# Up weights of two units loaded together by rows, and up products of the last 128 tokens over 512 columns at a time

## The chip, the cores and the metric

The kernel runs on one core of one Trainium2 chip. The metric is device time in microseconds (us), the median of repeated runs. Before the change it is 1033.2 us (three runs, 1032.21 to 1035.63). A profiled execution is a run of its own, with its own time.

## The reference

Attention with a linear memory, then a softplus feed-forward layer, then a mixture of eight experts whose gates are balanced by Sinkhorn rounds. All of it is in fp32.

```python
x = attention(q, k, v, M_prev, z_prev, beta)      # 1152 tokens x 512
g = softplus(x @ w_in)                            # w_in 512 x 2048
x = g @ w_out                                     # 1152 x 512
P = sinkhorn(x @ w_gate)                          # 1152 x 8, eight rounds
for e in range(8):
    h = np.maximum(x @ w1[e], 0.0)                # w1[e] 512 x 1024
    out += P[:, e:e + 1] * (h @ w2[e])            # w2[e] 1024 x 512
```

## The kernel before, in words

Each fp32 operand is split in two fp32r parts: a high part (`...h`, copied and rounded by ACT) and a low part (`...l`, the rest, subtracted by DVE). A product takes three matmuls: high by high, high by low, low by high.

The 1152 tokens are three chunks, 512, 512 and 128. The two chunks of 512 go together through a Strassen form of seven block products (`product`, L1264: 42 matmuls of 512 columns in a unit); their weights are the four blocks a11, a21, a12, a22 of a unit and four sums s1 to s4 of these. The last chunk, 128 tokens, is done plainly (`plain`, L1285): its tokens are the stationary side, and the weights are the moving side.

The experts' work is a list of units. An expert has two halves `s`; a half has two up units (`what` = 2s and 2s+1, each for 256 hidden columns) and one down unit that uses the hidden values of both. `up2` does an up unit: products of A, C and B in turn, and between them ACT's copies of A (`keep`, L1327) and DVE's additions of C to them (L1331). `plain` stands between the third product and the fourth and fifth, and writes its unit's 256 columns of the PSUM bank `po`; after the second unit of a half `hidden` (L1309) copies the bank, transposes it and splits it.

Weights come in by `load_pair` (L1147): one DMA of 512 KB into one of two `raw` buffers, then four jobs: split of row 0 (a11, a21), sums s1 and s2 (POOL) and their split, split of row 1 (a12, a22), sums s3 and s4 and their split. A unit's load stands LOOK = 3 units ahead in a list of jobs (`pump_q`), from which `pump()` takes one between products. A split part lies in a `slot` of 128x512, out of a ring of W0 + W1 = 27 (the first 16 in use from the start, 11 more after the attention), taken in order and free when the last matmul has read it.

Nothing of this order is fixed by hand: `Plan` lists every instruction with what it reads and writes, and a list scheduler places them, engine by engine, with the planner's own cost for each. The engines then run their queues in that order and wait on semaphores.

Of the kernel before, what the change touches and what calls it, by code (L numbers as in the profile page):

```python
# [19 lines left out]
P = 128  # L20
# [6 lines left out]
E = 8  # L27
# [10 lines left out]
GROUPS = [list(range(n, n + 4)) for n in range(0, 16, 4)]  # L38
AT = (14, 16, 18, 20)
AO = (34, 36, 38, 39)  # L40
W0, W1 = 16, 11
HT, HG, HH, HU, HS = 4, 8, 12, 8, 2
LOOK = 3
YIELD = 80
# [46 lines left out]
        self.ap = pool.tile(self.shape, self.dtype, name=self.name, **kw)  # L91


class Op:
    __slots__ = ("eng", "ns", "fn", "rank", "wait", "outs", "ready", "allocs", "touch", "start", "lat", "end", "port", "kind")


class Plan:
# [17 lines left out]
    def add(self, eng, ns, fn, r=(), w=(), lat=0, rank=None, after=(), port=False, kind=None):  # L116
        o = Op()
        o.eng, o.ns, o.fn, o.lat, o.port, o.kind = eng, ns, fn, lat, port, kind
        self.rank += 1
        o.rank = self.rank + self.shift if rank is None else rank  # L120
        o.outs, o.ready, o.allocs, o.touch, deps = [], 0, [], {}, set(after)
        for bufs, write in ((r, False), (w, True)):
            for b in bufs:
                b, sub = b if isinstance(b, tuple) else (b, None)
                for s, p, pw in b.log:
                    if p is not o and (write or pw) and (
                            s is None or sub is None or s == sub or s[0] != sub[0]):
                        deps.add(p)
                b.log.append((sub, o, write))
                if write and b not in o.allocs:  # L130
                    o.allocs.append(b)
                    if b.pool in self.gates:
                        deps.add(self.gates[b.pool])
                o.touch[b] = True
        o.wait = len(deps)
        for p in deps:
            p.outs.append(o)
        self.ops.append(o)
        return o
# [111 lines left out]
def fused_kernel(ctx, tc, kq, vq, gm, w_in, w_out, wg, w1, w2, out1, out2):  # L251
# [22 lines left out]
    def pe(ns, fn, r, w, **kw):  # L274
        return pl.add("PE", ns, fn, r, w, kind=kw.pop("kind", "all"), **kw)
# [11 lines left out]
    def dma(kb, fn, w, r=(), late=0, **kw):  # L287
        return pl.add("SP", max(460, kb * 2.8), fn, r, w, lat=2000 + late + kb * 2.8, **kw)
# [27 lines left out]
    pl.banks["slot"] = [(None, ("w", f"w{n}")) for n in range(W0)]  # L316

    def slot(name):
        return pl.any_buf("slot", [P, 512], F32R, name)

    def load_split64(src, name, after=(), psum=False, keep=False):
        raw = pl.buf("d", [P, 512, 2], U32, "raw64", "raw")
        a = pl.buf("psb", [P, 512], F32, "cv", "b5") if psum else pl.buf("d", [P, 512], F32, "wa", "wa")
        hi, lo = slot(name + "h"), slot(name + "l")
# [32 lines left out]
    def sum_moe1(g, k):  # L359
# [12 lines left out]
        op(s12, R, s12, L, one, L, ALU.subtract)  # L372
        op(s34, R, two, L, s12, R, ALU.subtract)
        for n, t in enumerate((s12, s34)):
            hi, lo = slot(f"s{g}{k}{n}h"), slot(f"s{g}{k}{n}l")
# [769 lines left out]
    wa_, wb_, wd_ = {}, {}, {}  # L1145

    def load_pair(src, e, i, order, rows, table):  # L1147

        box = []
        at = {name: slice(n * 256, (n + 1) * 256) for n, name in enumerate(order)}  # L1150

        def two(ap, read, name, lo_eng):
            hi, lo = slot(name + "h"), slot(name + "l")
            copy(512, lambda: hi.ap, ap, read, [hi])
            pair(512, lambda: lo.ap, ap, lambda: hi.ap.bitcast(F32), ALU.subtract, [*read, hi], [lo], eng=lo_eng)
            return hi, lo

        def load():
            raw = pl.buf("d", [P, 1024], F32, "raw", "raw")
            box.append(raw)  # L1160
            dma(512, lambda: nc.sync.dma_start(raw.ap, src[e, i]), [raw])

        def row(r):
            raw = box[0]
            hi, lo = two(lambda: raw[:, r * 512:(r + 1) * 512], [raw], f"a{e}{i}{r}", "DVE")
            if rows is not None:
                rows[e, i + 4 * r] = hi, lo
            for m in range(2):
                table[e, i, order[2 * r + m]] = hi, lo, m

        def sums(r):
            raw = box[0]
            t = pl.buf("d", [P, 512], F32, "ws", "wa")

            def op(m, x, y, o, rd):
                pair(256, lambda: t[:, m * 256:(m + 1) * 256], x, y, o, rd, [t])

            def a(name):
                return lambda: raw[:, at[name]]

            if r == 0:
                op(0, a("a21"), a("a22"), ALU.add, [raw])
                op(1, lambda: t[:, 0:256], a("a11"), ALU.subtract, [raw])
                box.append(t)
            else:
                q = box[1]
                op(0, a("a11"), a("a21"), ALU.subtract, [raw])
                op(1, a("a12"), lambda: q[:, 256:512], ALU.subtract, [raw, q])
            hi, lo = two(lambda: t.ap, [t], f"s{e}{i}{r}", "DVE")
            for m in range(2):  # L1190
                table[e, i, f"s{2 * r + m + 1}"] = hi, lo, m

        return [load, lambda: row(0), lambda: sums(0), lambda: row(1), lambda: sums(1)]

    def load_unit(n):
        e, s, what = units[n]
        if what != "down":
            return load_pair(w1, e, what, ("a11", "a21", "a12", "a22"), None, wa_)
        two = [load_pair(w2, e, i, ("a11", "a21", "a12", "a22"), wb_, wd_) for i in (2 * s, 2 * s + 1)]
        return [f for fs in two for f in fs]  # L1200

    pr = pl.buf("cst", [P, NTT, E], F32, "pr")

# [80 lines left out]

    def plain(o, e, i):  # L1285


        n = i % 2
        out = slice(n * 256, (n + 1) * 256)

        def step(k):
            wh, wl, _ = wa_[e, i, "a1%d" % (k // 2 + 1)]
            h, l = xh[2], xl[2]

            def cols(w):
                return w.ap.rearrange("p (r k f) -> p k r f", r=2, k=2)[:, k % 2]

            def mm():
                kw = {"skip_group_check": True} if n else {}
                nc.tensor.matmul(o[:, out], h[:, k, :], cols(wh), start=(n + k == 0), stop=False, **kw)  # L1300
                nc.tensor.matmul(o[:, out], h[:, k, :], cols(wl), start=False, stop=False, **kw)
                nc.tensor.matmul(o[:, out], l[:, k, :], cols(wh), start=False, stop=(k == KD - 1), **kw)

            pe(3 * mms(256), mm, [wh, wl, h, l], [o])

        for k in range(KD):
            step(k)

    def hidden(o):  # L1309
# [226 lines left out]
def _layout(q, k, v, M_prev, z_prev, beta, moe_w_in, moe_w_out, moe2_w_gate, moe2_w1, moe2_w2):  # L1536
# [16 lines left out]
    for j in range(2):  # L1553
# [12 lines left out]
        "wg": c(moe2_w_gate.reshape(KD, P, E).transpose(1, 0, 2)),  # L1566


        "w1": c(moe2_w1.reshape(E, 2, 2, P, 2, NF2 // 2, P).transpose(0, 5, 3, 1, 4, 2, 6)).reshape(E, NF2 // 2, P, 1024),
# [21 lines left out]
```

## Time and profile before

| | |
|---|---|
| median of the runs | 1033.2 us |
| the profiled execution, its own time | 1032.61 us |
| its span, first to last instruction | 1030.8 us |
| PE / DVE / ACT / POOL busy | 1017.0 / 916.8 / 593.6 / 342.7 us |
| attention and start of the first layer | 0 to about 125 us |
| feed-forward layer | about 125 to 310 us |
| experts | about 310 us to the end |

The busy time of PE (matmuls) is drawn from modelled ends: a 512-column matmul is shown as 0.39 us long while the next one starts 0.227 us later. What a matmul takes of PE is therefore read from the starts of successive matmuls. The clock column PEclk gives the granted share of TensorE's full clock; 1.00 is 2.4 GHz.

### The profile page before, as it was taken

To read this page: it belongs to the slowest core of one execution; us is meant where nothing else is said; L and a number is where in the kernel's file an instruction comes from. 1 tells how busy PE (TensorE), PEld (TensorE's weight loads), DVE (VectorE), ACT (ScalarE), POOL (GpSimd) and SP (SyncE) were. 2 spreads that over 40 slices of the span, in tenths; PEclk is the share of its full clock that TensorE was granted. 3 is DMA by queue.
4 is the path that set the end of the run, shared out by engine and by line. 5 is a ranking of instruction groups with operands and counts; after the bars stand their busy time and mean duration, and the time that the engine had idled before them with its cause. 6 is when DMAs were issued, how large, how long until landed. Compare 5 with 4: busy or idle time off the path is not lost.

```text
span 1030.8 us, 14822 instructions
## 1 busy us (share of the span) xinstructions
PE 1017.0 (99%) x5270; PEld 836.0 (81%) x5270; DVE 916.8 (89%) x1722; ACT 593.6 (58%) x1200; POOL 342.7 (33%) x360
## 2 busy tenths in 40 slices
PE   7999999999999999999999999999999999999998
PEld 5777787888877888888888888888888888888886
DVE  7998877767668999999999999999999999999987
ACT  6888877766756764546454553545545344553542
POOL 3424351313343233433323333242432323343220
PEclk9999999999999999999999999999999999999999
DMA  4340222332201112211111211211211121111102
GB/s 167 126 152 26 87 82 82 103 102 102 103 21 41 42 56 59 62 62 61 62 41 53 71 42 62 62 41 42 73 50 41 62 62 62 40 54 62 41 2 92
DMA packets 27021, 68.38 MB, mean 66 GB/s; under 512 B 2556, under 2 KB 11332, under 8 KB 26948
## 3 DMA queue, kind: packets, MB, share of 16 engines
q1 hardware_dynamic: 26948, 67.45, 20.0%
q8 instruction: 41, 0.67, 0.3%
q14 instruction: 32, 0.26, 0.1%
HBM read 65.04 MB, written 2.40 MB: 65 GB/s over the span
## 4 chain that ended last, share of the span: by engine, by line
PE 93%; DVE 3%; ACT 3%; issue 1%; DMA 0%; ACTq 0%; DVEq 0%
PE pa L1276 6%; PE pa L1277 6%; PE pa L1278 6%; PE dA L1451 6%; PE dA L1450 6%; PE dA L1452 6%; PE pc L1278 3%; PE pc L1276 3%; PE pc L1277 3%; PE dn L919 3%; PE dn L918 3%; PE dn L917 3%; PE dC L1451 3%; PE dC L1450 3%; PE dC L1452 3%; PE xp L683 2%
## 5 line engine op out<-in xcount | busy, mean ns | idle before, releaser
L284 POOL TENSOR_TENSOR ws<-raw 128x256 f32<-128x256 f32 x128 | 122.8, 959 | 450.0 <-issue 104.5
L279 ACT ACTIVATE fh<-u 128x512 fp32r<-128x512 f32 x160 | 99.3, 628 | 121.7 <-DVE u L1376 65.5
L285 DVE TENSOR_TENSOR fl<-u,fh 128x512 fp32r<-128x512 f32 x160 | 110.9, 694 | 1.9 <-ACT fh L279 1.8
L1327 ACT ACTIVATE u<-pa 128x512 f32<-128x512 f32 x64 | 38.0, 593 | 66.4 <-PE pa L1278 65.9
L1467 DVE TENSOR_TENSOR acc<-dA,acc 128x512 f32<-128x512 f32 x92 | 62.3, 681 | 4.9 <-PE dA L1452 4.8
L1347 ACT ACTIVATE pb<-pa 128x512 f32<-128x512 f32 x32 | 18.6, 582 | 78.8 <-PE pa L1278 53.1
L284 POOL TENSOR_TENSOR ws<-raw,ws 128x256 f32<-128x256 f32 x64 | 61.8, 966 | 0.0
L279 ACT ACTIVATE fh<-t 128x512 fp32r<-128x512 f32 x64 | 38.6, 624 | 37.3 <-DVE t L1376 37.3
L284 POOL TENSOR_TENSOR ws<-ws,raw 128x256 f32<-128x256 f32 x64 | 57.3, 896 | 4.9
L1331 DVE TENSOR_TENSOR u<-pc,u 128x512 f32<-128x512 f32 x64 | 43.9, 686 | 7.6 <-ACT u L1327 5.5
L285 DVE TENSOR_TENSOR fl<-t,fh 128x512 fp32r<-128x512 f32 x64 | 47.3, 740 | 0.0
L1340 DVE SCALAR_TENSOR_TENSOR u<-u,pb 128x512 f32<-128x512 f32 x56 | 42.5, 759 | 0.6
L1467 DVE TENSOR_TENSOR acc<-dC,acc 128x512 f32<-128x512 f32 x62 | 40.1, 679 | 0.3
L593 ACT ACTIVATE pr<-pr,mn 128x128 f32<-128x128 f32 (+3 forms) x64 | 35.6, 560 | 7.5 <-DVE mn L578 7.3
L279 ACT ACTIVATE pt<-tp 128x512 f32<-128x512 f32 (+3 forms) x72 | 31.2, 451 | 6.6 <-PE tp L607 6.2
L570 PE MATMUL sp<-st 64*128 64x256 f32 (+2 forms) x192 | 26.7, 383 | 6.6 <-ACT st L279 5.1
L683 PE MATMUL xp<-pt,vt 128*64 128x128 f32 (+2 forms) x480 | 32.1, 265 | 0.0
L284 POOL TENSOR_TENSOR gl<-u,gh 128x512 fp32r<-128x512 f32 x12 | 15.5, 1295 | 49.1 <-ACT u L844 49.1
L578 DVE CUSTOM_DVE_ANT_0 pr<-sp,mask 128x128 f32<-128x128 f32 (+3 forms) x64 | 29.6, 483 | 2.3 <-PE sp L570 2.0
L607 PE MATMUL tp<-ident,pr 128*128 128x128 f32 x160 | 28.9, 290 | 1.8 <-DVE pr L624 0.8
L333 DVE SCALAR_TENSOR_TENSOR cv<-cv,raw 128x512 uint32<-128x512 uint32 x24 | 16.7, 696 | 15.7 <-ACT raw L331 15.7
L284 POOL TENSOR_TENSOR st<-kqd,st 128x640 fp32r<-128x640 f32 (+1 forms) x14 | 21.2, 1529 | 23.6 <-ACT st L279 23.6
(5131 smaller groups left out, 3600.7 us busy)
## 6 DMA issues: line engine op xcount, KB each, us to landing
raw<-w SPq DMA_DIRECT2D x64, 512.0 KB, 3.4
raw<-w_in SPq DMA_DIRECT2D x16, 512.0 KB, 3.5
raw<-w_out SPq DMA_DIRECT2D x16, 512.0 KB, 3.5
vt<-vq SPq DMA_DIRECT2D x8, 608.0 KB, 4.0
kqd<-kq SPq DMA_DIRECT2D x7, 608.0 KB, 4.1
pb<-gates SPq DMA_DIRECT2D x16, 256.0 KB, 5.1
out<-acc SPq DMA_DIRECT2D x9, 256.0 KB, 2.0
gms<-gm SPq DMA_DIRECT2D x2, 260.0 KB, 6.1
```

The lines of the kernel that those rows point to most:

```text
L279: return act(n, lambda: nc.scalar.activation(out(), src(), AF.Copy), r, w, x=-42 if psum else 0, **kw)
L284: return gps(n, lambda: nc.gpsimd.tensor_tensor(out=out(), in0=a(), in1=b(), op=op), r, w, **kw)
L285: return dve(n, lambda: nc.vector.tensor_tensor(out=out(), in0=a(), in1=b(), op=op), r, w, port=True, **kw)
L683: nc.tensor.matmul(xp[j * D:(j + 1) * D, P - R:P], vt[:kk, t * P + j * D:t * P + (j + 1) * D], src, start=False, stop=(t == nb - 1), skip_ ...
L1276: nc.tensor.matmul(o[:, :CH], wh[:, at], h(), start=start and k == 0, stop=False, **kw)
L1277: nc.tensor.matmul(o[:, :CH], wh[:, at], l(), start=False, stop=False, **kw)
L1278: nc.tensor.matmul(o[:, :CH], wl[:, at], h(), start=False, stop=(k == 1), **kw)
L1331: dve(CH, lambda: nc.vector.tensor_tensor(out=t.ap, in0=o[:, :CH], in1=t.ap, op=ALU.add), [o], [t], rank=pl.rank - FORE)
L1450: nc.tensor.matmul(o[:, :CH], wh[:, at], h.ap, start=start and n == 0, stop=False, **kw)
L1451: nc.tensor.matmul(o[:, :CH], wh[:, at], l.ap, start=False, stop=False, **kw)
L1452: nc.tensor.matmul(o[:, :CH], wl[:, at], h.ap, start=False, stop=(n == 1), **kw)
L1467: dve(CH, lambda: nc.vector.tensor_tensor(out=acc[c][:, cs_], in0=o[:, :CH], in1=acc[c][:, cs_], op=ALU.add), [o], [a_])
```

## The change

The up weights of a half (two units) are laid out by rows: one 512 KB DMA brings a row block (a11, a21 or a12, a22) of both units. `load_up` issues the two DMAs at the first unit; each unit then has its own four jobs, so both `raw` buffers stay in use until the second unit's last job. The down weights are loaded as before, by `load_down`.

The ring has tiles of 128x1024: W0 = 8 and W1 = 5, 13 doubles in place of 27 singles. For up rows a double holds the high (or the low) part of one row for both units, and becomes free only when both units are done with it; for sums, down rows and the first layer's weights it holds high and low part of one row. `Half` lets the planner treat the two halves apart when it looks for dependencies.

`plain` runs over 512 columns, those of both units: two of the four k steps in the first unit and two in the second (for the first half of the first expert all four in the second unit). A half's 24 matmuls of 256 columns become 12 of 512, with a moving operand of four pieces of 128 columns, where there were two.

```diff
-W0, W1 = 16, 11
+W0, W1 = 8, 5
...
     def slot(name):
-        return pl.any_buf("slot", [P, 512], F32R, name)
+        return pl.any_buf("slot", [P, 1024], F32R, name)
+
+    def two_parts(name):
+        s = slot(name)
+        return Half(s, 0), Half(s, 1)
...
+    def load_up(e, s):
+        raws = []
 
         def load():
-            raw = pl.buf("d", [P, 1024], F32, "raw", "raw")
-            box.append(raw)
-            dma(512, lambda: nc.sync.dma_start(raw.ap, src[e, i]), [raw])
+            for r in range(2):
+                load_raw(raws, w1[e, s, r])
+                wp_[e, s, r] = slot(f"a{e}{s}{r}h"), slot(f"a{e}{s}{r}l")
+
+        def row(n, r):
+            i = 2 * s + n
+            hi, lo = [Half(w, n) for w in wp_[e, s, r]]
+            parts_of(lambda: raws[r][:, n * 512:(n + 1) * 512], [raws[r]], hi, lo)
+            for m in range(2):
+                wa_[e, i, BLOCKS[2 * r + m]] = hi, lo, m
...
+            return [lambda: row(n, 0), lambda: sums_of(e, 2 * s + n, 0, raws, blk, kept, wa_),
+                    lambda: row(n, 1), lambda: sums_of(e, 2 * s + n, 1, raws, blk, kept, wa_)]
+
+        return [[load, *unit(0)], unit(1)]
...
     def plain(o, e, i):
...
-            wh, wl, _ = wa_[e, i, "a1%d" % (k // 2 + 1)]
+            wh, wl = wp_[e, i // 2, k // 2]
             h, l = xh[2], xl[2]
 
             def cols(w):
-                return w.ap.rearrange("p (r k f) -> p k r f", r=2, k=2)[:, k % 2]
+                return w.ap.rearrange("p (q k f) -> p k q f", q=4, k=2)[:, k % 2]
 
             def mm():
-                kw = {"skip_group_check": True} if n else {}
-                nc.tensor.matmul(o[:, out], h[:, k, :], cols(wh), start=(n + k == 0), stop=False, **kw)
...
+                nc.tensor.matmul(o.ap, h[:, k, :], cols(wh), start=(k == 0), stop=False)
...
-        for k in range(KD):
+        for k in (() if i == 0 else range(KD)) if e == 0 and i < 2 else range(i % 2 * 2, i % 2 * 2 + 2):
             step(k)
```

The planner then places everything anew. Up to the feed-forward layer's last group the order on PE is as it was. Two places of the experts follow, both in the first half of expert 3 (numbers behind names are buffer numbers).

PE in the first unit, before: the last three rows of `plain` (`po`), what follows them, and the first rows of the a22 product (`pa` written from a301).

```order
L1300 MATMUL po_6727<-a301h_6443,xh2_1445 128x256
L1301 MATMUL po_6727<-a301l_6468,xh2_1445 128x256
L1302 MATMUL po_6727<-a301h_6443,xl2_1459 128x256
L1276 MATMUL pa_6750<-xh0_287,a310h_6487 128x512
L1277 MATMUL pa_6750<-xl0_300,a310h_6487 128x512
L1278 MATMUL pa_6750<-xh0_287,a310l_6524 128x512
L1276 MATMUL pa_6518<-xs20h_2421,a301h_6443 128x512
L1277 MATMUL pa_6518<-xs20l_2473,a301h_6443 128x512
L1278 MATMUL pa_6518<-xs20h_2421,a301l_6468 128x512
```

The same place now: the last three rows of `plain` in this unit (of six), and what follows.

```order
L1346 MATMUL po_6504<-a300h_6150,xh2_1441 128x512
L1347 MATMUL po_6504<-a300l_6169,xh2_1441 128x512
L1348 MATMUL po_6504<-a300h_6150,xl2_1455 128x512
L1327 MATMUL pa_6325<-xs20h_2412,a301h_6231 128x512
L1328 MATMUL pa_6325<-xs20l_2463,a301h_6231 128x512
L1329 MATMUL pa_6325<-xs20h_2412,a301l_6265 128x512
L1327 MATMUL pc_6426<-xh1_497,s301_6274 128x512
L1328 MATMUL pc_6426<-xl1_505,s301_6274 128x512
L1329 MATMUL pc_6426<-xh1_497,s301_6274 128x512
```

The three matmuls of the next unit (a310) that stood between `plain` and the a22 product have moved away, and twelve short `plain` rows are now six long ones.

DVE where the same unit's `pc` is added to the copy `u3` (L1331 before), before: what stands in front of the addition, and behind.

```order
L285 TENSOR_TENSOR a310l_6716<-raw_6586,a310h_6711 128x512
L1340 SCALAR_TENSOR_TENSOR u1_6725<-pb_6599,pb_5606 128x512
L285 TENSOR_TENSOR s310l_6731<-ws_6693,s310h_6718 128x512
L1331 TENSOR_TENSOR u3_6738<-pc_6571,u3_6738 128x512
L1340 SCALAR_TENSOR_TENSOR u3_6738<-u3_6738,pb_6445 128x512
L285 TENSOR_TENSOR a311l_6767<-raw_6586,a311h_6733 128x512
```

The same place now (L1377 is the addition).

```order
L1513 TENSOR_TENSOR acc0_2365<-dA_6240,acc0_2365 128x512
L299 TENSOR_TENSOR a310_6489<-raw_6381,a310_6489 128x512
L1377 TENSOR_TENSOR u3_6508<-pc_6426,u3_6508 128x512
L299 TENSOR_TENSOR s310_6495<-ws_6469,s310_6495 128x512
L1386 SCALAR_TENSOR_TENSOR u3_6508<-u3_6508,pb_6245 128x512
L299 TENSOR_TENSOR fl_6523<-u1_6471,fh_6477 128x512
```

A split of down weights (a310) stands directly in front of the addition now, and the split of s310 behind it, where both stood in front of it.

## Rows read from the trace of the kernel before

**Rows 1.** Page, part 1: busy us, share of the span, instructions of each engine.

```profile
span 1030.8 us, 14822 instructions
PE 1017.0 (99%) x5270; PEld 836.0 (81%) x5270; DVE 916.8 (89%) x1722; ACT 593.6 (58%) x1200; POOL 342.7 (33%) x360
```

**Rows 2.** Page, part 4: the chain that ended last, by engine.

```profile
PE 93%; DVE 3%; ACT 3%; issue 1%; DMA 0%; ACTq 0%; DVEq 0%
```

**Rows 3.** Stretches (us), busy us and instructions by engine, PEclk, DMA share, GB/s.

```profile
0.00:125.00 125.00, 115.41 (x1039) 86.56 (x1040) 110.72 (x436) 102.08 (x307) 45.53 (x56) 1.00 0.34 115
125.00:290.00 165.00, 164.49 (x762) 135.38 (x760) 119.60 (x188) 117.01 (x214) 55.30 (x51) 1.00 0.27 91
290.00:420.00 130.00, 129.83 (x620) 105.56 (x619) 114.91 (x223) 76.86 (x138) 44.63 (x45) 1.00 0.17 49
420.00:1000.00 580.00, 580.00 (x2729) 486.03 (x2729) 548.08 (x842) 287.23 (x524) 197.20 (x209) 1.00 0.16 52
```

**Rows 4.** Waits of PE, 125 to 1031 us: us in total, times, longest.

```profile
PE pa L821 <- ACT pb L853: 0.5, 1, 0.5
PE dA L1451 <- DVE fl L285: 0.2, 1, 0.2
```

**Rows 5.** The stretch 290 to 1031 us, line L1300 alone: PE and weight loads.

```profile
290.00:1031.00 741.00, 36.40 (x128) 24.40 (x128) 1.00 0.16 53
```

**Rows 6.** PE in order of time, around one plain block: start, length, line.

```profile
468.80 0.39 PE L1276 MATMUL pa<-xh,s131h 128*128 128x512 f32 x1
...
470.16 0.28 PE L1300 MATMUL po<-a130h,xh 128*128 128x256 f32 x1
...
471.60 0.40 PE L1276 MATMUL pa<-xs20h,a131h 128*128 128x512 f32 x1
```

**Rows 7.** Page, part 6: weight loads, count, KB, us to landing.

```profile
raw<-w SPq DMA_DIRECT2D x64, 512.0 KB, 3.4
```

**Rows 8.** Waits of the DMA queue, 420 to 1000 us.

```profile
SPq L1161 <- DVE a421l L285: 23.0, 2, 11.9
```

**Rows 9.** Tile a420l: who writes and reads it, first and last start.

```profile
L285 DVE TENSOR_TENSOR a420l<-raw,a420h x2: 674/679/684, 691.2 to 719.2; 128x512 fp32r<-128x512 f32 x2
...
L1278 PE MATMUL pa<-xh,a420l x2: 389/389/389, 703.1 to 703.8; 128*128 128x512 f32 x2
```

**Rows 10.** PE in order of time, another plain block.

```profile
558.35 0.39 PE L1278 MATMUL pa<-xh,s231l 128*128 128x512 f32 x1
558.58 0.28 PE L1300 MATMUL po<-a230h,xh 128*128 128x256 f32 x1
...
560.01 0.40 PE L1276 MATMUL pa<-xs20h,a231h 128*128 128x512 f32 x1
```

**Rows 11.** ACT at the same place.

```profile
558.84 0.60 ACT L1327 ACTIVATE u<-pa 128x512 f32<-128x512 f32 x1
```

**Rows 12.** DVE at the same place.

```profile
559.23 0.69 DVE L285 TENSOR_TENSOR fl<-u,fh 128x512 fp32r<-128x512 f32 x1
559.83 0.69 DVE L1331 TENSOR_TENSOR u<-pc,u 128x512 f32<-128x512 f32 x1
```

**Rows 13.** Waits of DVE, 420 to 1000 us.

```profile
DVE u L1340 <- PE pb L1278: 7.9, 9, 1.1
DVE acc L1416 <- PE dy L1404: 5.7, 6, 1.0
```

More of the change, by code (lines that the diff above doesn't have):

```diff
@@ L123, in add @@
             for b in bufs:
+                if isinstance(b, Half):
+                    b = b.buf, ("half", b.n)
                 b, sub = b if isinstance(b, tuple) else (b, None)
@@ L1144, in fused_kernel @@
     units = [(e, s, what) for e in range(E) for s in range(2) for what in (2 * s, 2 * s + 1, "down")]
[L1145 to L1156, printed above, removed]
-        def load():
-            raw = pl.buf("d", [P, 1024], F32, "raw", "raw")
-            box.append(raw)
-            dma(512, lambda: nc.sync.dma_start(raw.ap, src[e, i]), [raw])
+    wa_, wb_, wd_, wp_ = {}, {}, {}, {}
@@ new lines, in load_up, with unit, blk @@
+    def load_up(e, s):
+        raws = []
+        def load():
+            for r in range(2):
[5 more added lines that the diff above has]
+            parts_of(lambda: raws[r][:, n * 512:(n + 1) * 512], [raws[r]], hi, lo)
+            for m in range(2):
+                wa_[e, i, BLOCKS[2 * r + m]] = hi, lo, m
+        def unit(n):
+            kept = []
+            def blk(name):
+                k = BLOCKS.index(name)
+                at = n * 512 + k % 2 * 256
+                return raws[k // 2][:, at:at + 256]
+            return [lambda: row(n, 0), lambda: sums_of(e, 2 * s + n, 0, raws, blk, kept, wa_),
+                    lambda: row(n, 1), lambda: sums_of(e, 2 * s + n, 1, raws, blk, kept, wa_)]
+        return [[load, *unit(0)], unit(1)]
@@ L1163, in row, with load_down, blk @@
+    def load_down(e, i):
+        raws, kept = [], []
+        def blk(name):
+            k = BLOCKS.index(name)
+            return raws[0][:, k * 256:(k + 1) * 256]
         def row(r):
[L1164 to L1167, printed above, removed]
+            hi, lo = wb_[e, i + 4 * r] = two_parts(f"a{e}{i}{r}")
+            parts_of(lambda: raws[0][:, r * 512:(r + 1) * 512], raws, hi, lo)
@@ L1168, in row @@
             for m in range(2):
[L1169 to L1191, printed above, removed]
@@ L1193, in load_pair @@
-        return [load, lambda: row(0), lambda: sums(0), lambda: row(1), lambda: sums(1)]
+                wd_[e, i, BLOCKS[2 * r + m]] = hi, lo, m
+        return [lambda: load_raw(raws, w2[e, i]), lambda: row(0), lambda: sums_of(e, i, 0, raws, blk, kept, wd_),
+                lambda: row(1), lambda: sums_of(e, i, 1, raws, blk, kept, wd_)]
+    odd = {}
     def load_unit(n):
         e, s, what = units[n]
-        if what != "down":
-            return load_pair(w1, e, what, ("a11", "a21", "a12", "a22"), None, wa_)
@@ L1199, in load_unit @@
-        two = [load_pair(w2, e, i, ("a11", "a21", "a12", "a22"), wb_, wd_) for i in (2 * s, 2 * s + 1)]
-        return [f for fs in two for f in fs]
+        if what == "down":
+            return [f for i in (2 * s, 2 * s + 1) for f in load_down(e, i)]
+        if what % 2:
+            return odd.pop((e, s))
+        first, odd[e, s] = load_up(e, s)
+        return first
     pr = pl.buf("cst", [P, NTT, E], F32, "pr")
```

47 lines of the change are left out of this document (39 added, 8 removed).

## The prediction

> **What bounds the kernel now.** I read the page's busy times first, then the chain of waits, then the stretches, then the waits of PE, and last the order of time around `plain`. PE is busy 1017.0 of 1030.8 us and makes up 93% of the chain that ended last [rows 1, 2]. The stretches say where: up to 125 us PE lacks 9.6 us, since attention has waits of its own; from 420 to 1000 us, where the experts run, it is busy for 580.00 of 580.00 us at the full clock of 2.4 GHz (PEclk 1.00) [rows 3]. Busy ends are modelled, so I check this by the waits: from 125 us to the end PE waits twice, 0.5 and 0.2 us [rows 4]. So PE is a queue without holes, and whatever is taken out of the queue moves the end by as much, as long as nobody who feeds PE comes late. DVE is the one to watch: 548.08 of 580 us busy, 94.5% [rows 3], and some of the rest is waits on PE (7.9 and 5.7 us are the largest) [rows 13]. ACT has half its time free, 287 of 580 us, POOL two thirds.
>
> **The change part by part.**
>
> *The plain products.* L1300 runs 128 times [rows 5], and L1301 and L1302 stand in the same step, so 384 matmuls of 256 columns go. 16 halves x 4 steps x 3 make 192 of 512 columns that come. What a matmul takes is the distance of starts: twelve of 256 columns run from 470.16 to 471.60, 0.120 us each, and the six of 512 ahead of them from 468.80 to 470.16, 0.2267 us each [rows 6]. So 384 x 0.120 = 46.1 us go and 192 x 0.2267 = 43.5 us come: 2.6 us less. Columns are the same in number; what goes is a fixed part, 2 x 0.120 - 0.2267 = 0.013 us, 192 times.
>
> No row shows a 512-column matmul whose moving side is four pieces of 128. From below it is the contiguous one, 0.2267 us. From above it is two of the old ones, 0.240 us, each with two such pieces; then the gain is nothing. I take 0.2267, since the old ones with two pieces already fit the same line: 0.2267 less 0.120 is 0.1067 us for 256 columns, 2.4 columns a ns, the full clock, and 0.013 us is left over in both.
>
> The Trainium skill, page "TensorE: Matmul & The Clock Gate", section "Back-to-back issue gap", gives the warm distance as columns over 2.4 plus about 2.5 ns. By that, an estimate from the page, the fixed part is 2.5 ns, the change would take out 192 x 2.5 ns = 0.5 us, and the time would be within 0.1% of before. The trace does not agree: it has 13 ns left over at both sizes [rows 6], and the measurement decides.
>
> *Splits, sums and DMAs.* Each of them is as many and as large as before: 64 loads of 512 KB, landing after 3.4 us [rows 7], the same ACT copies, DVE subtractions and POOL sums of 512 and 256 columns. Cost: 0 in work. They move: both row blocks of a half are loaded at its first unit, and both `raw` buffers are held until the second unit's last sum. The loads were held up by `raw` before as well (23.0 us in two waits behind one split of DVE, up to 11.9 us each) [rows 8], and nobody downstream noticed, because the splits run far ahead: a420l, among the closest in the steady part, is written at 691.2 us and first read at 703.1, 11.9 us later [rows 9]. That lead is the cover for three edits together: the later `raw`, the double tiles that become free only after both units, and the ring of 26 halves where there were 27 slots. I put them at 0. `plain` now reads the second unit's row 0 one unit early, and in the new order DVE makes the splits of both units' row 0 one after the other, ahead of that. Bounds: below nothing there is only the 0.7 us of PE's own waits to gain [rows 4]; above, a lead that fell short by one load would cost 3.4 us each time [rows 7], but it would first have to lose the 11.9 us.
>
> *The copies behind a shorter filler.* `plain` hides ACT's copy of `pa`, which must be done before the a22 product writes that bank. Before, it took 1.44 us (12 x 0.120) and in places 0.68 us more (three matmuls of the next unit, as in the first piece of PE's order above). Now it is 6 x 0.2267 = 1.36 us, with nothing behind it in the first unit; in the second unit it is three `plain` rows and three of a down product, 1.36 us too. The trace shows what has to fit: with the last `pa` product started at 558.35 and `plain` at 558.58 [rows 10], ACT's copy starts at 558.84 and takes 0.60, to 559.44 [rows 11], and the a22 product starts at 560.01: 0.57 us to spare with 1.43 us of filler. With 1.36 it is 0.50 us. Cost 0, as long as ACT is free when `pa` is ready.
>
> *The addition behind it.* In the first unit the `pc` product follows 0.68 us after the filler, so DVE's addition has 1.36 + 0.68 = 2.04 us from the start of `plain`. In the same example DVE did it from 559.83 to 560.52, 1.94 us after 558.58 [rows 10, 12], because a split stood in front of it until then. That fits by 0.1 us. If the addition starts as soon as ACT is done, it ends near 559.44 + 0.69 = 560.13, which leaves 0.5 us. I put it at 0, with little room.
>
> *The tail and the start.* PE's order up to the last group of the feed-forward layer is the same row for row; nothing is gained or lost there. The place between 290 and 420 us, where the gates are computed, gets a new order; PE lacks 0.17 us there [rows 3], so a gain is at most that and a loss perhaps 0.5 us, one ACT wait like the one in rows 4.
>
> *Sum.* 1032.61 us, the profiled execution's own time (span 1030.8 and 1.8 around it), less 2.6 is 1030.0. The median of the runs shown lies 0.6 above that execution, so 1030.6.
>
> **The rivals.**
>
> *The fixed part isn't saved.* If the 13 ns belong to pieces or to something a half's 512 columns pay as well, the new matmul takes 0.240 us, the sum is 0 and the time 1033.2. For it: no row has four pieces. Against it: 512 contiguous columns and 256 in two pieces lie on one line [rows 6].
>
> *PE waits for DVE's addition in each half.* The mechanism is the shorter filler above: in the new order a split of down weights stands directly in front of the addition, and it waits itself for ACT's copy of the same weights. If it starts one DVE row late (0.60 us from 559.23 to 559.83 [rows 12]), the addition ends 0.60 - 0.1 = 0.5 us after PE wants `pc`, in each of 16 halves: 8.0 us, 1038.6 us, slower. At 2.6 / 16 = 0.16 us a half it cancels the gain; from (2.6 + 3.1) / 16 = 0.36 us a half it is slower by over 0.3%. For it: DVE is at 94.5%, and the filler loses 0.08 to 0.76 us. Against it: in front of the addition stood two splits before, now one. A part of it, 0.05 to 0.15 us in each half, would leave 1031.4 to 1033.
>
> *The ring starves the loads.* If doubles come free so late that a split's lead is gone, PE waits for weights: 3.4 us for a load, in the worst case in each half, 54 us. For it: a double waits for two units. Against it: 11.9 us of lead. I give this almost nothing.
>
> **How the numbers follow.** A measurement of this kernel tells about 0.3% from no change, 3.1 us; 1030.1 is the border. Forecast, gain of 2 to 3.3 us: 0.65, its own range 1029.4 to 1031.4. Fixed part not saved: 0.10, at 1032.6 to 1033.5. Small waits eat part or all of it: 0.11, 1031.4 to 1033.5. DVE's addition late in each half, 1036 and more: 0.12; the starved ring: 0.02. The forecast of 1030.6 lies 0.25% below the median of before, just inside the border; with the spread of the runs some 0.34 of the chance falls below 1030.1. Slower by over 0.3% is 0.13, and the rest, 0.53, is within. The range from 1028.9 to 1034.2 holds the forecast, the unsaved fixed part and the small waits; the late addition lies outside.
>
> **What would show each step right or wrong.** In the new profile, six `plain` matmuls should span 1.36 us, and their line should have 64 instructions where L1300 has 128; a span of 1.44 us is the first rival. From 420 to 1000 us the waits of PE should stay near nothing; a wait of `pc` on DVE's `u`, some 16 times, is the second rival, and waits of PE on splits of `a` or `s` the third. DVE's busy time should be the same 917 us within 1. The feed-forward layer and the attention should end where they did. The forecast is wrong if the span differs from 1028.2 by more than 1.2 us, and the reasoning is wrong if it is right with waits in PE that something else paid for.

## The result, and the profile after

The changed kernel takes 1038.2 us (median of six runs, 1037.7 to 1039.44) against 1032.7 of the kernel before in the same job: a ratio of 1.0054, 95% interval 1.0038 to 1.007. The forecast was 1030.6 and the range ended at 1034.2, so it was wrong in sign as well.

The page, part 1, and the chain by engine:

```profile
span 1037.7 us, 14552 instructions
...
PE 1019.5 (98%) x5078; PEld 825.1 (80%) x5078; DVE 902.2 (87%) x1722; ACT 605.4 (58%) x1200; POOL 340.6 (33%) x360
...
PE 90%; DVE 4%; ACT 2%; DMA 1%; issue 1%; POOL 1%; SPq 0%; ACTq 0%; POOLq 0%; DVEq 0%
```

PE has 192 matmuls fewer [rows 1], and yet the span is 6.8 us longer. Its share of the chain fell by three points [rows 2]. The stretches, in the columns of [rows 3]:

```profile
0.00:125.00 125.00, 115.20 (x1028) 86.35 (x1030) 109.54 (x434) 101.43 (x304) 45.10 (x56) 0.99 0.33 112
125.00:290.00 165.00, 164.05 (x766) 134.59 (x763) 120.00 (x188) 117.42 (x216) 52.52 (x48) 1.00 0.27 89
290.00:420.00 130.00, 127.92 (x579) 101.45 (x578) 110.03 (x214) 77.44 (x137) 45.82 (x45) 1.00 0.15 47
420.00:1000.00 580.00, 578.32 (x2562) 474.87 (x2561) 533.49 (x843) 296.46 (x523) 197.16 (x212) 1.00 0.17 54
```

PE now has holes from 290 to 420 us (127.92 for 129.83 before) and from 420 to 1000 (578.32 for 580.00). DVE is *less* busy there than before, 533.49 for 548.08. PE's waits from 125 us to the end:

```profile
PE pa L1327 <- ACT pb L1393: 1.2, 1, 1.2
PE pa L839 <- ACT pb L871: 0.9, 1, 0.9
PE dC L1497 <- DVE fl L299: 0.5, 1, 0.5
PE dA L1496 <- DVE acc L1513: 0.4, 1, 0.4
PE dA L1497 <- DVE fl L299: 0.2, 1, 0.2
```

Five short waits against two [rows 4] don't add up to the loss: short stalls are hidden by the modelled ends. The distance of starts shows them. The first `dy` product stands at the same place of each half, here of two halves late in the run, now and then before:

```profile
881.76 0.39 PE L1448 MATMUL dy<-a,hh 128*128 128x512 f32 x1
...
926.13 0.39 PE L1448 MATMUL dy<-a,hh 128*128 128x512 f32 x1
```

```profile
875.41 0.39 PE L1402 MATMUL dy<-a600h,hh 128*128 128x512 f32 x1
...
919.62 0.39 PE L1402 MATMUL dy<-a620h,hh 128*128 128x512 f32 x1
```

A half takes 44.37 us; before it was 44.21 (875.41 to 919.62), and the shorter plain products should have made it 44.05. So there is a regular stall of some 0.3 us a half. Most of the rest of the loss lies in the passage from the first to the second expert, near 410 to 420 us; 0.6 us is lost in the first layer already, near 172 us, where the wait of `pa` on `pb` is 0.9 us now and was 0.5 [rows 4].

The plain products themselves do what they should; the line has 64 instructions [rows 5], and the starts are 0.227 us apart [rows 6]:

```profile
564.46 0.39 PE L1346 MATMUL po<-a211h,xh 128*128 128x512 f32 x1
564.68 0.39 PE L1347 MATMUL po<-a211l,xh 128*128 128x512 f32 x1
564.91 0.39 PE L1348 MATMUL po<-a211h,xl 128*128 128x512 f32 x1
565.13 0.39 PE L1496 MATMUL dA<-fh,a 128*128 128x512 f32 x1
```

Now the regular stall. First PE around it, where 0.51 us lie between two starts in place of 0.23; then DVE; then POOL (`ws` is a sum of weight blocks):

```profile
585.79 0.39 PE L1498 MATMUL dC<-fh,s 128*128 128x512 f32 x1
586.30 0.47 PE L1496 MATMUL dA<-fh,s 128*128 128x512 f32 x1
```

```profile
583.11 0.69 DVE L299 TENSOR_TENSOR fl<-u,fh 128x512 fp32r<-128x512 f32 x1
583.72 1.23 DVE L299 TENSOR_TENSOR s<-ws,s 128x512 fp32r<-128x512 f32 x1
584.87 0.68 DVE L299 TENSOR_TENSOR fl<-u,fh 128x512 fp32r<-128x512 f32 x1
585.48 0.68 DVE L1513 TENSOR_TENSOR acc<-dA,acc 128x512 f32<-128x512 f32 x1
```

```profile
583.55 0.85 POOL L298 TENSOR_TENSOR ws<-raw 128x256 f32<-128x256 f32 x1 [3.06 <-DMA raw<-w]
```

The `dA` product overwrites a bank that DVE's addition `acc<-dA` must have read, and that addition ends at 586.16. It is late because one row ahead of it, `s<-ws`, took 1.23 us in place of 0.69: POOL's sum had begun 0.17 us earlier, the moment its `raw` landed. DVE has no idle time from 580.7 on, so the 0.54 us reach the addition whole. Of them PE loses 0.36 us a half: 0.28 at this start and 0.08 at the next.

Such stretched rows are nothing new. Before, DVE had 51 rows of over 0.95 us from 420 to 1000 us in the trace, now 17. One of before, DVE and the POOL row beside it:

```profile
638.89 1.23 DVE L285 TENSOR_TENSOR a331l<-raw,a331h 128x512 fp32r<-128x512 f32 x1
640.39 0.69 DVE L1331 TENSOR_TENSOR u<-pc,u 128x512 f32<-128x512 f32 x1 [0.27 <-PE pc L1278]
```

```profile
638.50 1.07 POOL L284 TENSOR_TENSOR ws<-raw 128x256 f32<-128x256 f32 x1 [1.30 <-DVE s330l L285]
```

There the row behind the stretched one waits for PE anyway, and nothing is lost. The question for the experiments was whether one of 17 such rows costs more than all 51 of before.

### The profile page after: what moved, and what is told of

Same layout as the page of the kernel before. It is cut to its first block, busy times and chain, and to the rows that moved or that the text cites. A ratio compares the mean times of both kernels' runs of the same rounds, so it can differ in the third digit from the quotient of the medians.

```text
span 1037.7 us, 14552 instructions
## 1 busy us (share of the span) xinstructions
PE 1019.5 (98%) x5078; PEld 825.1 (80%) x5078; DVE 902.2 (87%) x1722; ACT 605.4 (58%) x1200; POOL 340.6 (33%) x360
## 4 chain that ended last, share of the span: by engine, by line
PE 90%; DVE 4%; ACT 2%; DMA 1%; issue 1%; POOL 1%; SPq 0%; ACTq 0%; POOLq 0%; DVEq 0%
PE dA L1496 6%; PE pa L1327 6%; PE pa L1329 5%; PE pa L1328 5%; PE dA L1497 5%; PE dA L1498 5%; PE pc L1327 3%; PE pc L1329 3%; PE pc L1328 3%; PE dn L937 3%; PE dn L935 3%; PE dn L936 3%; PE dC L1497 3%; PE dC L1498 3%; PE dC L1496 3%; PE xp L701 2%
## 5 line engine op out<-in xcount | busy, mean ns | idle before, releaser
L293 ACT ACTIVATE s<-ws 128x512 fp32r<-128x512 f32 x128 | 80.3, 628 | 139.9 <-PE dA L1498 85.6
L299 DVE TENSOR_TENSOR s<-ws,s 128x512 fp32r<-128x512 f32 x128 | 95.3, 744 | 0.3 <-ACT s L293 0.3
L1377 DVE TENSOR_TENSOR u<-pc,u 128x512 f32<-128x512 f32 x64 | 44.1, 689 | 32.4 <-ACT u L1373 24.7
L293 ACT ACTIVATE a<-raw 128x512 fp32r<-128x512 f32 x64 | 40.0, 625 | 52.4 <-PE pc L1329 36.5
L1496 PE MATMUL dA<-fh,s 128*128 128x512 f32 x128 | 51.0, 399 | 1.7 <-DVE acc L1513 0.4
L1497 PE MATMUL dC<-fl,s 128*128 128x512 f32 x128 | 49.9, 390 | 0.5 <-DVE fl L299 0.5
L1496 PE MATMUL dA<-fh,a 128*128 128x512 f32 x128 | 50.3, 393 | 0.1
L1497 PE MATMUL dA<-fl,a 128*128 128x512 f32 x128 | 50.0, 391 | 0.2 <-DVE fl L299 0.2
L935 PE MATMUL dn<-gh,wo 128*128 128x512 f32 x128 | 50.1, 391 | 0.0
L1497 PE MATMUL dA<-fl,s 128*128 128x512 f32 x128 | 50.0, 390 | 0.0
L1496 PE MATMUL dC<-fh,s 128*128 128x512 f32 x128 | 49.9, 390 | 0.0
L1498 PE MATMUL dA<-fh,a 128*128 128x512 f32 x128 | 49.9, 390 | 0.0
L1498 PE MATMUL dA<-fh,s 128*128 128x512 f32 x128 | 49.9, 389 | 0.0
L937 PE MATMUL dn<-gh,wo 128*128 128x512 f32 x128 | 49.8, 389 | 0.0
```

Source lines behind the costliest of these rows:

```text
L293: return act(n, lambda: nc.scalar.activation(out(), src(), AF.Copy), r, w, x=-42 if psum else 0, **kw)
L299: return dve(n, lambda: nc.vector.tensor_tensor(out=out(), in0=a(), in1=b(), op=op), r, w, port=True, **kw)
L935: nc.tensor.matmul(o.ap, wh[:, ds_], gh.ap, start=(n == 0), stop=False)
L937: nc.tensor.matmul(o.ap, wl[:, ds_], gh.ap, start=False, stop=(n == len(fs) - 1))
L1496: nc.tensor.matmul(o[:, :CH], wh[:, at], h.ap, start=start and n == 0, stop=False, **kw)
L1497: nc.tensor.matmul(o[:, :CH], wh[:, at], l.ap, start=False, stop=False, **kw)
```

## The experiments

"Half" is the time between the first `dy` starts of two halves late in the run (919.62 - 875.41 = 44.21 before); "long rows" are DVE's rows over 0.95 us from 420 to 1000 us. Ratios are to runs of the kernel before in the same job.

| run | us | ratio, 95% | half | long rows |
|---|---|---|---|---|
| before | 1032.7 to 1033.4 | | 44.21 | 51 |
| the change | 1038.2 | 1.0054 (1.0038 to 1.007) | 44.37 | 17 |
| e1_doubles | 1034.13 | 1.0009 (1.0 to 1.0018) | 44.23 | 27 |
| e2_rows | 1032.72 | 0.9996 (0.9988 to 1.0005) | 44.22 | 74 |
| e3_unit512 | 1039.21 | 1.0058 (1.0045 to 1.007) | 44.01 | 52 |
| e4_ring14 | 1051.01 | 1.017 (1.0156 to 1.0184) | 44.71 | 60 |
| e5_after256 | 1038.54 | 1.0052 (1.0038 to 1.0066) | 44.24 | 50 |
| e6_pb4 | 1039.31 | 1.0068 (1.0056 to 1.0081) | 44.41 | 17 |
| e7_raw3 | 1056.17 | 1.0225 (1.0211 to 1.0239) | 45.40 | 61 |
| e8_pool32 | 1030.45 | 0.9975 (0.9965 to 0.9985) | 44.01 | 0 |
| e9_pad | 1031.43 | 0.9989 (0.998 to 0.9998) | 44.01 | 0 |
| e10_before32 | 1032.70 | 1.0 (0.9991 to 1.0009) | 44.21 | 0 |
| e11_late512 | 1031.80 | 0.9988 (0.9979 to 0.9997) | 44.01 | 50 |
| e12_late512rows | 1036.33 | 1.0033 (1.0021 to 1.0046) | 44.37 | 15 |
| e13_one_sum | 1033.54 | 0.9999 (0.999 to 1.0008) | 44.00 | 4 |
| e14_unit32 | 1036.98 | 1.0032 (1.002 to 1.0045) | 44.00 | 0 |

**One part at a time (e1 to e3), and more ring (e4).** e1 is the kernel before with the ring of doubles; rows are still loaded unit by unit:

```diff
-W0, W1 = 16, 11
+W0, W1 = 8, 5
...
-        hi, lo = slot(name + "h"), slot(name + "l")
+        hi, lo = two_parts(name)
```

> The kernel before with one part of the change: the ring of double tiles (8 + 5, a high and a low half in one tile); the up weights are still loaded unit by unit and the plain products still stand over 256 columns. Against 1032.7 us of the kernel before. Theory 'ring' (13 doubles, freed in pairs, leave ScalarE's copies waiting for a tile): 1036 to 1041, with ACT L293-like copies waiting for PE some 50 us and more. Theory 'raw' (both raw buffers are held across two units): within 1 us of before, since the raw buffers are used as before. Theory 'order' (any new order of the planner costs some us somewhere): anywhere from 1031 to 1038, with no tie to the waits for a ring tile.

e2 is the kernel before with `load_up`'s two DMAs for two units, single slots and 256 columns:

```diff
-            dma(512, lambda: nc.sync.dma_start(raw.ap, src[e, i]), [raw])
+            for r in range(2):
+                load_raw(raws, w1[e, s, r])
```

> The kernel before with another part alone: the up weights loaded by rows, two raw loads for two units, with the old ring of 27 single tiles and the plain products over 256 columns. Theory 'raw': the whole loss without the 2.6 us that the wider plain products give back, 1038 to 1041, with the sync engine's waits for a raw buffer at 250 us and more in 420 to 1000 and the sums on GpSimd waiting for raw loads. Theory 'ring': 1032.7, within 1 us. Theory 'order': 1031 to 1038, no tie to the raw waits.

e3 is the changed kernel with `load_raw(raws, w1[e, i])` at each unit:

```diff
-            for r in range(2):
-                load_raw(raws, w1[e, s, r])
+            load_raw(raws, w1[e, i])
```

> The changed kernel with the up weights loaded unit by unit as before (one raw buffer each, freed by its unit), but with the ring of doubles, the row tiles shared by two units and the plain products over 512 columns. Theory 'raw': the 2.6 us of the plain products and nothing else, 1029 to 1031. Theory 'ring': 1037 to 1039, as the changed kernel. A third theory, 'filler' (the shorter plain products leave a late addition uncovered): also 1037 to 1039, with the stall at the same places in each half. Theory 'order': anything from 1030 to 1037.

```diff
-W0, W1 = 8, 5
+W0, W1 = 8, 6
```

> The changed kernel with one double tile more from the gate on (8 + 6, 14 doubles instead of 13); to make room for it the gate's rows lie in a tile of the u ring and the gate's weights in another pool. Theory 'ring': most of the loss goes, 1030 to 1034, and ScalarE's waits for a ring tile fall from 82 us to under 30. Theory 'raw': no change, 1037 to 1039, and the sync engine's waits for raw buffers stay at some 500 us. Theory 'order': 1033 to 1040.

'Raw' fell with e2: the by-rows loads alone cost nothing. 'Ring' fell with e1 (1 us) and with e4, where one tile more cost 13 us more. e3 has halves of 44.01, so the gain of the plain products is there and the regular stall is gone, but by 486 us it has lost some 8 us (against e8 below). No single part carries the loss. 'Order' was left, which explains nothing by itself: every edit re-plans all lists. So the next runs keep the lists.

**The plain products undone (e5).** `plain` as before, on the shared double tiles.

```diff
-                nc.tensor.matmul(o.ap, h[:, k, :], cols(wh), start=(k == 0), stop=False)
+                nc.tensor.matmul(o[:, out], h[:, k, :], cols(wh), start=(n + k == 0), stop=False, **kw)
```

> The changed kernel with the plain products over 256 columns again: double row tiles shared by two units, loads by rows and the ring of 13 doubles stay. Theory 'shared rows' (the four doubles of a pair, held until its second unit has ended, leave the ring short): the changed kernel's loss stays and the 2.6 us come on top, 1039 to 1042. Theory 'filler' (the shorter plain products leave DVE's additions uncovered): the loss goes, 1032 to 1034. Theory 'order' (each list of instructions has stalls of its own): 1033 to 1042, at other places than in the changed kernel.

It is as slow as the changed kernel, at other places (PE waits 2.6 us for ACT's copy of `po`; halves of 44.24). So the wider plain products are not needed for a loss of this size. But the stall in each half is gone here, and e5 alone can't say whether the old filler or the new lists took it away; e8 and e13 below do, since they keep the shorter filler and have no stall.

**The same lists with more buffers (e6, e7).** The planner's order is that of the changed kernel; only the pools rotate over more buffers. (For room, e7 puts three small tiles of the gates in other places.)

```diff
-            kw["bufs"] = self.plan.bufs[self.pool, self.tag]
+            kw["bufs"] = {("h2", "pb"): 4}.get((self.pool, self.tag), self.plan.bufs[self.pool, self.tag])
```

> The changed kernel, every engine's list of instructions word for word the same, with four buffers for the gate rows pb instead of three, so that the sync engine's load of the fourth pb no longer waits and the raw load behind it in the queue goes out earlier. Theory 'queue' (the stalls near 410 to 417, some 2 us, come of raw loads that stand behind pb loads on the sync engine): 1035.5 to 1037. If the late raw loads of the passage to the second expert have another cause: 1038, within 0.7 us of the changed kernel. The regular stall of each half, 0.3 us, stays in either case.

```diff
+            kw["bufs"] = {("d", "raw"): 3}.get((self.pool, self.tag), self.plan.bufs[self.pool, self.tag])
```

> The changed kernel, every engine's list of instructions in the same order, with three raw buffers instead of two. Theory 'raw': raw loads land some us earlier, GpSimd's sum no longer falls on DVE's split of a sum in the last quarter of a half, the regular stall of 0.36 us in each of some 12 halves goes: 1033 to 1035. Theory 'sums' (GpSimd's sums, wherever they fall, stretch a DVE split that the next dA product waits for): the stall moves or stays, 1036 to 1039. Theory 'ring' (ScalarE waits for a ring tile): no change, 1038.

e6 doesn't test its question, and its 1039.31 us lie outside both ranges: the fourth `pb` load went out 20 us earlier, but the fifth, also ahead of the `raw` load in SP's queue, still waited, and that `raw` load went out at 424.50. e7 was expected to help and cost 18 us more. Loads that land earlier start POOL's sums earlier; 61 DVE rows are long now, and the regular stall is a new one, PE waiting for ACT's copy of `pa`:

```profile
PE pa L1327 <- ACT u L1373: 3.9, 12, 1.3
```

**POOL's sums made short, or harmless (e8 to e10).** The lists stay the same again. In e8 and e10 a sum covers 32 of 256 columns; in e9 it does too, and then POOL writes a constant over the rest.

```diff
-            pair(256, lambda: t[:, m * 256:(m + 1) * 256], x, y, o, rd, [t])
+            pl.add("POOL", 160 + 2.2 * 256, lambda: nc.gpsimd.tensor_tensor(
+                out=t[:, m * 256:m * 256 + 32], in0=x()[:, :32], in1=y()[:, :32], op=o), rd, [t], port=True)
```

> The changed kernel, lists of instructions in the same order, with GpSimd's sums of the experts' weights over 32 columns instead of 256 (the splits behind them read these 32 columns eight times; this leaves most of the sums out), so that they hardly overlap a VectorE instruction. Theory 'sums': VectorE's splits take 0.69 us everywhere, the regular stall of 0.36 us a half goes, and with it 4 to 5 us: 1033 to 1035. Theory 'raw' or 'ring' (transfers or a ring tile come late): 1037 to 1038.5, the regular stall stays.

```diff
+                for _ in range(2):
+                    nc.gpsimd.memset(t[:, at + 32:at + 256], 0.0)
```

> As the run before it with sums over 32 columns (the splits read these eight times; most of the sums is left out), lists in the same order, and behind each such sum GpSimd writes a constant twice over the other 224 columns of the tile, so that it is busy about as long as with a whole sum (some 0.8 us) but reads nothing from SBUF in that time. Theory 'shared reads' (the loss is VectorE's instruction with two SBUF inputs held up while GpSimd reads SBUF): VectorE has next to no instruction over 0.95 us in 420 to 1000, and the time is 1029.5 to 1032. Theory 'late sums' (the loss is the sums' own length: raw buffers, ws tiles and ring tiles come free later): back to 1036 to 1039.

> The kernel before, lists in the same order, with GpSimd's sums of the experts' weights over 32 columns instead of 256 (the splits read these eight times; most of the sums is left out). If the sums cost nothing in the kernel before, although 51 of VectorE's instructions in 420 to 1000 are stretched there: 1031.5 to 1033.5, halves of 44.2 us as before. Then the whole of the 8 us by which the same edit made the changed kernel faster is a cost of the change. If the sums cost as much before: 1025 to 1028.

The stretch 420 to 1000 us of e8, of e9 and of e10, columns as above:

```profile
420.00:1000.00 580.00, 580.00 (x2585) 480.02 (x2584) 527.77 (x847) 297.02 (x524) 73.44 (x210) 1.00 0.17 53
```

```profile
420.00:1000.00 580.00, 580.00 (x2585) 480.02 (x2584) 528.57 (x848) 296.51 (x525) 196.42 (x631) 1.00 0.17 53
```

```profile
420.00:1000.00 580.00, 580.00 (x2730) 486.04 (x2729) 519.85 (x841) 287.12 (x526) 85.36 (x208) 1.00 0.16 52
```

This settles the main point. With short sums the changed kernel takes 1030.45 us, below the 1033 to 1035 expected and near the forecast; the same edit does nothing for the kernel before (1032.70). In e9 POOL is as busy as in the changed kernel (196.42 for 197.16 us), but no DVE row is long, PE is busy for 580.00 of 580, and the time is 1031.43. So it isn't the length of the sums but DVE's rows held up beside them: some 7 of the 7.8 us between the changed kernel and e8. The other 1 us is in the passage (389 to 435 us), where PE stops for 0.6 us in e9 and not in e8: in e9 a copy of ACT waits 0.88 us there for POOL, and the copy that PE needs stands behind it.

**One sum in sixteen (e13).** Only the first sum of the even down block is made harmless, in the way of e9; 240 of 256 sums stay.

```diff
+            if one and n == m == 0:
+                def go():
+                    nc.gpsimd.tensor_tensor(out=t[:, 0:32], in0=x()[:, :32], in1=y()[:, :32], op=o)
+                    for _ in range(2):
+                        nc.gpsimd.memset(t[:, 32:256], 0.0)
```

> The changed kernel, lists in the same order, with one of GpSimd's sixteen sums per half made harmless: the first sum of the even down block is done over 32 columns, and a constant is written twice over the other 224, which takes as long and reads nothing (this leaves that part of the sums out). Theory 'one sum' (it alone stretches VectorE's split of a sum at 583.72, 628.08, ...): halves of 44.0 to 44.1 us instead of 44.37 from the sixth on, and 1033 to 1035.5 in all, since the losses of the passage to the second expert may stay. Theory 'all sums' (many sums add up): halves of 44.25 us and more, 1036.5 to 1038.5.

The place of the regular stall in e13: POOL, DVE, PE, and the first `dy` of the halves shown above.

```profile
582.12 0.39 POOL L1182 TENSOR_TENSOR ws<-raw 128x32 f32<-128x32 f32 x1 [3.03 <-DMA raw<-w]
582.45 0.62 POOL L1184 MEMSET ws<- 128x224 f32 x2
```

```profile
582.32 0.74 DVE L299 TENSOR_TENSOR s<-ws,s 128x512 fp32r<-128x512 f32 x1
582.98 0.68 DVE L299 TENSOR_TENSOR fl<-u,fh 128x512 fp32r<-128x512 f32 x1
583.59 0.68 DVE L1521 TENSOR_TENSOR acc<-dA,acc 128x512 f32<-128x512 f32 x1
```

```profile
584.40 0.39 PE L1506 MATMUL dC<-fh,s 128*128 128x512 f32 x1
584.62 0.39 PE L1504 MATMUL dA<-fh,s 128*128 128x512 f32 x1
...
877.74 0.39 PE L1456 MATMUL dy<-a,hh 128*128 128x512 f32 x1
...
921.74 0.39 PE L1456 MATMUL dy<-a,hh 128*128 128x512 f32 x1
```

POOL starts as late as before and is as long, but DVE's row takes 0.74 us, the addition is done in time, PE doesn't stop, and the half is 44.00. One sum in sixteen carries some 5 us of the loss: 4.7 by the medians, 5.7 by the two ratios (e13 ran on another chip), 4.8 in the traces from the second expert's first `dy` to the last half's. Against e8 some 3 us remain; by the first `dy` starts 2.1 of them lie in the passage, and 0.8 in the half before it, where PE stops near 348 us for a `fl` row that DVE took 1.22 us for in the changed kernel. What happens in the passage, in the changed kernel, is ACT, then DVE, then PE:

```profile
408.00 0.63 ACT L293 ACTIVATE a<-raw 128x512 fp32r<-128x512 f32 x1 [5.08 <-DMA raw<-w]
409.99 0.63 ACT L293 ACTIVATE s<-ws 128x512 fp32r<-128x512 f32 x1 [1.36 <-POOL ws L298]
410.52 0.61 ACT L293 ACTIVATE a<-raw 128x512 fp32r<-128x512 f32 x1
411.04 0.58 ACT L1393 ACTIVATE pb<-pa 128x512 f32<-128x512 f32 x1
```

```profile
410.42 1.75 DVE L299 TENSOR_TENSOR a<-raw,a 128x512 fp32r<-128x512 f32 x1
412.20 1.12 DVE L299 TENSOR_TENSOR fl<-u,fh 128x512 fp32r<-128x512 f32 x1
413.24 1.77 DVE L299 TENSOR_TENSOR acc<-acc,pb 128x512 f32<-128x512 f32 x1
```

```profile
411.67 0.50 PE L1327 MATMUL pa<-xs10h,s 128*128 128x512 f32 x1 [1.17 <-ACT pb L1393]
```

ACT's copy of `pa`, which PE needs at once, stands in ACT's queue behind weight copies that nobody needs yet, and these wait for a late `raw` load and for POOL. That load went out at 398.70 and landed at 407.9, after 9.2 us instead of 3.4, beside three `pb` loads of which the last landed at 406.6. DVE rows are long there as well. The late load alone is not the cause: in e8 it took as long (396.78 to 406.24), and PE doesn't stop there. What differs is POOL: from the copy at 408.00 to the copy of `s`, which waits for two sums, it is 1.99 us here, 1.51 in e9 and 0.70 in e8.

**The passage with unit loads (e14).** e3 with the edit of e8.

> The changed kernel with unit loads (e3), lists in the same order, with GpSimd's sums over 32 columns (the splits read these eight times; most of the sums is left out). Theory 'shared reads': the 7 us of the passage to the second expert go, 1029.5 to 1032. Theory 'queue' (raw loads behind the gate rows' loads on the sync engine come late): the 4.9 us stall near 433 stays, 1036 to 1039.

The sums are not the main cause here: 1036.98 us is only 2.2 less than e3, and the stall that e3 had at 432.67 stays, 4.3 us for 4.7. PE's wait, ACT behind it, and the waits of SP's queue from 410 to 440 us:

```profile
PE dA L1504 <- DVE fl L299: 4.3, 1, 4.3
```

```profile
430.67 0.62 ACT L293 ACTIVATE fh<-u 128x512 fp32r<-128x512 f32 x1
433.99 0.63 ACT L293 ACTIVATE a110h<-raw 128x512 fp32r<-128x512 f32 x1 [2.71 <-DMA raw<-w]
434.53 0.61 ACT L293 ACTIVATE fh<-t 128x512 fp32r<-128x512 f32 x1
```

```profile
SPq L1319 <- DVE acc L299: 15.2, 2, 14.2
SPq L1174 <- DVE a L299: 9.5, 2, 8.3
```

A copy of up weights waits for its `raw` load, and the `fh` copy behind it in ACT's queue is what DVE, and then PE, wait for. That load went out at 430.49, when DVE had freed its buffer; the load ahead of it had gone out at 421.73, behind two `pb` loads that waited for DVE's `acc` rows (417.20 in the kernel before). So by the trace the stall in e3 comes of a late load; no run moved that load alone, and how much of its lateness is the `pb` loads and how much the `raw` buffer isn't separated, since e6 missed its mark.

**A version that beats both (e11, e12).** Rows shared by two units and 512 columns only from the third expert on; e11 with unit loads, e12 by rows.

```diff
+        if e < 2:
+            for k in range(KD):
+                half(k)
+            return
```

> A mix that could beat both: ring of 13 doubles, up weights loaded unit by unit, and only from the third expert on the row tiles shared by two units with the plain products over 512 columns; the first two experts have row tiles of their own and plain products over 256 columns. If the losses of the kernel with unit loads lie in the passage from the first to the second expert alone: halves of 44.0 us from the third expert on and 1031 to 1032.5. Theory 'order' (the new order of the third expert's passage has stalls of its own): 1033 to 1039.

> The same mix with the changed kernel's loads by rows. If the one-off losses go with the first passage and the halves of 44.37 us stay: 1035.5 to 1037. If the halves come out at 44.0: 1030 to 1032. Theory 'order': up to 1040.

e11 has the halves of e3 (44.01), loses 0.9 us in the passage to the second expert (45.12 us from `dy` to `dy` for 44.23 before; e3 loses 6.2 there and in the half behind it), and takes 1031.80 us: 0.12% under before (interval 0.03% to 0.21%, so barely clear of noise) and 6 us under the change. That 50 of its DVE rows are long does no harm. e12 has the changed kernel's halves of 44.37, so the regular stall, and 1036.33 us.

## Why the prediction was wrong

**The plain products: right.** 192 matmuls at 0.227 us and 64 instructions on the line; where nothing else interferes (e3, e8, e13) a half takes 0.20 us less than before, for 0.16 forecast; the plain rows themselves take 0.14 of it. Between e10 and e8, which differ by the change alone with sums out of the way, lie 2.25 us (2.6 by the ratios) for 2.6. That this meets the forecast is partly luck: sixteen times 0.20 us is 3.2, and the first layer gives 0.6 of it back (see "Places at rest"). The first rival, the fixed part that isn't saved, is out, and the 13 ns hold for four pieces as well.

**"Splits, sums and DMAs ... I put them at 0": the step that failed.** It counted the rows, found them equal, and bounded what the new places could cost by the lead of the weights, 11.9 us [rows 9]. That lead held: no wait of PE on a weight is among the five. But it covers PE against late weights alone. The same jobs stand in the queues of DVE and ACT, which work in order, ahead of rows that PE waits for soon. A row that is stretched by 0.54 us, or waits for a load, delays those. The prediction gave no row a price for running *beside* another, although the trace of before holds 51 stretched rows, at 0.69 and 1.23 us, to take it from. Measured by e8 against the change, the step that stood at 0 is 7.8 us: some 5 of them one sum (e13 against the change), some 3 the passage and the half before it.

**"DVE at 94.5% is the one to watch": right engine, wrong reading.** Its busy time fell from 916.8 to 902.2 us (917 within 1 was forecast), and PE lost time on it all the same. Without stretched rows DVE is busy for 519.85 us from 420 to 1000 us in place of 548.08 (e10), and the time is the same: 28 us of the busy time of before had slack behind it, so the share said little either way.

**The second rival: near in number, wrong in mechanism.** It gave 1038.6 us for a `pc` product that waits for DVE's addition in each half. No such wait is in the list; the wait in each half is of `dA` on `acc<-dA`, at another place, and it costs 0.36 us and not 0.5. The shorter filler is not its cause, since e13 keeps the filler and loses the stall. That it named DVE's lateness in each half and 8 us was luck in the size. It had a chance of 0.12, and the range stopped short of it.

**The ring (third rival): not by that mechanism.** No wait of PE on a weight shows. Doubles alone cost 1 us (e1), of which 0.6 lie in the first layer; a tile more cost 13 us (e4), which no theory here foresaw.

**Places at rest.** The first `dn` product started 1.37 us later than before, with the same order in front of it; in e12, with the same order again, it was 1.39 us earlier, so this is the spread of executions and no part of the result. In the profiled execution of the changed kernel the granted clock was 0.51 from 75.0 to 78.5 us, the lower level, behind a wait of PE of 1.44 us in the attention; in those of before and of e12 it stayed at 1.00 there. What is part of the result comes after it: with the same order of products, PE loses 0.6 us near 172 us: 0.57 to 0.65 us in each of the 13 kernels with doubles and nothing more in the two others with single slots (e2, e10). So "nothing is gained or lost there" was wrong by this much. The place from 290 to 420 us was priced at "perhaps 0.5 us"; PE lacks 2.1 us there now.

What stays open is which part of the change puts the one sum on that DVE row. By-rows loads alone (e2), doubles alone (e1) and unit loads with all the rest (e3) each have lists of their own, and their halves (44.22, 44.23, 44.01 us) don't show the stall; nor do those of e5, with 256 columns. e12, where by-rows loads, shared doubles and 512 columns stand together from the third expert on, has it again. So it has shown only where all three stand together, and how they bring it isn't known. That the lists alone don't decide is shown by e7: the same lists, one buffer more, other collisions. What else e4 lost was not followed up.

## What to carry to other kernels

Price each row that moves by what it runs beside, not only by its own length: two engines that share a path to memory cost nothing while the delayed row has slack, and cost part of the delay (here 0.36 of 0.54 us) when a fed engine waits two rows later. A count of collisions, or a busy share, doesn't tell which it is; the rows between the stretched one and the next hand-over to the bottleneck do. When an edit re-plans every list, compare kernels with the same lists and one resource changed, and make the suspected work as long but harmless, before believing any part of the change guilty.

## What the runs showed of the hardware

A DVE row with two inputs in SBUF that starts while POOL adds two SBUF tiles ends 0.55 us after that sum does: with 0.68 us of the sum left it took 1.23 us instead of 0.69 (583.72 in the changed kernel), with 0.54 left 1.09 (510.03), with 0.14 left the usual 0.69 (552.34). In the kernel before, all 75 stretched rows of over 0.8 us from 420 to 1000 us end so. Such rows that start while POOL writes a constant took 0.67 to 0.69 us (e9, 420 to 1000 us), and rows with one input in PSUM at most 0.75 beside a whole sum (the changed kernel and e13). POOL's own sums of 256 columns are stretched as well, from 0.74 to 1.06 us and up to 1.25. The Trainium skill, page "SBUF — State Buffer", section "SBUF: two separate sides", has the rule: GpSimd and VectorE share one pair of ports, the first to start holds it for its whole instruction, and a VectorE instruction with two SBUF inputs is concerned only when the GpSimd one reads SBUF. By that rule e9 must come out like e8, and the trace agrees: no long row in either.

After the stop of 4.7 us in e3 the granted clock was 0.52, so the lower of the two levels (1.2 GHz), for eight matmuls 0.43 us apart, and then full again. Three stretches of e3, PE busy, PEclk, DMA share, GB/s:

```profile
432.00:437.70 5.70, 1.07 (x6) 1.00 0.26 93
437.70:441.20 3.50, 3.44 (x8) 0.52 0.00 0
441.20:446.00 4.80, 4.80 (x22) 0.99 0.36 109
```

That adds an estimated 8 x 0.2 = 1.6 us to what the stop itself cost.
